# A fused attention and feed-forward kernel: a pair of short blocks handled two pairs later, two squares moved between engines, and another order for the first block

## Chip, cores, metric

One core of a Trainium2 chip. The metric is the device time of one execution in microseconds (us), lower is better. Executions of this kernel scatter by about 1%, so differences of a few tenths of a per cent are read from traces, not from times. A trace's span is about 2 us shorter than the time of the same execution.

## The reference, cut to what matters

```python
# q, k, v: (8 batches, 8 heads, 576 positions, 64); x: 4608 tokens x 512
scores = scale * q @ k.T            # kept where 0 <= row - col < 64, else -1e9
attn = softmax(scores); y = attn @ v
x = y.transpose(0, 2, 1, 3).reshape(B * S, H * D)
h = np.maximum(x @ w_in, 0.0)       # w_in 512 x 2048
out = (h * h) @ w_out               # w_out 2048 x 512
```

A sequence of 576 positions is four blocks of 128 and one last block of 64. The last blocks of all eight sequences are gathered into two *pairs* of 128-token tiles (`TAILS`); a pair is 256 tokens, and there are 18 pairs.

## The kernel before: the parts that matter

Two pairs form a group of 512 tokens. Groups 0 and 1 are handled by a hand-written list of words, `FIRST`: `fk0` fetches the keys of pair 0, `kc1/D` casts keys of tile 1 on VectorE, `Tk0`/`ck0` transpose them and copy them out, `S0` makes the scores of tile 0, `V0` multiplies with the values, `X0`/`x0` make xT (the transposed activations), `w3.0` scales a quarter of w_in, `U0.7` is one projection of pair 0, `O` an output product, `W9` nine warm-up matmuls. The order of the words is the order on each engine and in the DMA queue. Every load, store and DMA transpose is issued by one queue, SyncE's, in that order.

From then on each *stage* g projects group g (`UP`), finishes group g-1 by a product scheme with sums on VectorE (`hsum`), does the attention of group g+1 and loads still later pairs. I number stages by g: stage 2 runs from its first `UP` to that of stage 3, and so on to stage 8.

```python
def UP(g, f):
    hps = ps_up.tile([P, 512], FP32, name="hps", tag="ps_u")      # two banks, used in turn
    for c in range(DMC):
        nc.tensor.matmul(hps[:], w_in_sb[:, c, f * P:(f + 1) * P], xT_of(g)[:, :, c, :], ...)   # L526
    hrelu = hrp.tile([P, 512], FP32, name="hrelu", tag="hrelu")
    nc.scalar.activation(out=hrelu[:], in_=hps[:], func=AF.Relu)                                # L530
    if f in SQ_ACT:         # the square reads hrelu alone: the bank is free after the relu
        later(2 if f == 0 else 0, lambda: nc.scalar.activation(
            out=h2_of(g)[:, f, :], in_=hrelu[:], func=AF.Square))                               # L533
    else:                   # the square reads hps too: the bank is free after the square
        nc.vector.scalar_tensor_tensor(out=h2_of(g)[:, f, :], in0=hps[:], scalar=0.0,
            in1=hrelu[:], op0=ALU.max, op1=ALU.mult)                                            # L536
...
# loads(p): dma_k, dma_q are the DMA transposes of keys and queries; load() fetches and casts
ev.append((t + 0.06, lambda a=a: (dma_k(a), dma_q(a))))
ev.append((t + 0.14, lambda a=a, x=kq: load(a + 1, x)))
ev.append((t + 0.3, lambda a=a, x=kq: load(a + 1, "kqv"[len(x):])))
...
# a pair of TAILS: 4 loads of keys, 4 of queries, 4 of values instead of 2, 2, 2;
# three DMA transposes instead of two; two stores (each the last 64 rows of two sequences) instead of one of 256 rows
```

The softmax here doesn't subtract the row's maximum and nothing guards it: scores larger than these inputs give would overflow.

## Time and profile before

| what | value |
|---|---|
| time | 297.83 us median of three (296.83 to 298.15) |
| profiled execution | 299.22 us, span 297.3 us: a longer one than those |
| TensorE | 96% busy, full clock |
| first projection (L498) | 19.85 us |
| first `UP` of stage 2 | 78.62 us |
| stages 2 to 7 | 32.24, 29.25, 28.88, 28.88, 29.88, 28.87 us |

The page of the kernel before: the engines' busy time, TensorE's busy tenths and granted clock in 40 slices, and the chain of waits by engine.

```profile
PE 284.6 (96%) x3042; PEld 196.5 (66%) x3042; DVE 218.8 (74%) x396; ACT 189.9 (64%) x300; POOL 119.7 (40%) x172
...
PE   4999999999989999999999999999999999999995
...
PEclk9999999999999999999999999999999999999999
...
PE 60%; DVE 16%; ACT 8%; DMA 7%; SPq 6%; issue 2%; POOL 1%; POOLq 0%
```

TensorE is nearly always busy, but only 60% of the chain that sets the time runs over it. The rest is where something else let it go on. The waits view of TensorE, before (what waited, on what: us in total, times, longest):

```profile
PE hps L526 <- DVE h L536: 3.1, 5, 1.0
PE warm L545 <- DVE mask_first L249: 2.7, 1, 2.7
PE kT_ps L373 <- DVE k L269: 1.6, 1, 1.6
...
PE sc L425 <- DMA qT<-q: 0.2, 1, 0.2
```

The largest wait after the start-up is `UP` on a VectorE square. One of the five in the timeline (start, duration, engine, line, operation, and in brackets the idle time before it and who ended it):

```profile
113.70 1.09 DVE L436 TENSOR_TENSOR pm<-pm,mask_inner 128x1024 f16<-128x1024 f16 x1
114.71 1.09 DVE L602 TENSOR_TENSOR hs_all<-h 128x1024 f16<-128x1024 f16 x1
115.84 0.69 DVE L602 TENSOR_TENSOR hs_all<-hs_all,h 128x1024 f16<-128x1024 f16 x1
116.45 0.68 DVE L536 SCALAR_TENSOR_TENSOR h<-hps,hrelu 128x512 f16<-128x512 f32 x1
...
113.86 0.59 ACT L530 ACTIVATE hrelu<-hps 128x512 f32<-128x512 f32 x1
115.43 0.60 ACT L530 ACTIVATE hrelu<-hps 128x512 f32<-128x512 f32 x1 [0.98 <-PE hps L526]
...
117.19 1.89 PE L526 MATMUL hps<-xT,w_in_sb 128*128 128x512 f16 x8 [0.29 <-DVE h L536]
```

The relu of f=1 (113.86) ended at 114.45, but its square stood behind a mask and two sums and ended at 117.13; only then could the next-but-one projection take the bank. ScalarE was idle for 0.98 us in between. (The view prints 0.29 us of idle; from the start of the matmul before, the gap over its own streaming time was 0.45. "By gaps" below means that.)

Last, the issuing queue around the start of stage 6 (197.87 us) in the kernel before, timeline of SyncE:

```profile
190.36 1.23 SPq L477 DMA_TRANSPOSE xT<-x_sb  x1
191.64 3.73 SPq L121 DMA_DIRECT2D kq_st<-in_q_dram  x4
195.41 3.54 SPq L121 DMA_DIRECT2D kq_st<-in_v_dram  x4
199.07 1.72 SPq L645 DMA_DIRECT2D out_dram<-osb_all  x2
200.88 0.73 SPq L651 DMA_DIRECT2D out_dram<-osb_all  x1
201.72 4.85 SPq L397 DMA_TRANSPOSE kT<-k  x2
206.66 2.20 SPq L397 DMA_TRANSPOSE qT<-q  x1
```

These follow one another without a gap. The last landed at 210.84 us, and the scores of that tile waited for it. I call the time from the start of the xT transpose to that landing the *stretch*: here 20.5 us.

One thing more is in the timeline at 113.70 to 116.5, and I overlooked it when I predicted: of operations of one shape (128x1024, fp16), some took 1.09 us and some 0.69.

### The profile page before, as it was taken

How to read it: one execution, taken by the hardware profiler on the slowest of the kernel's cores; microseconds unless marked ns; L12 is line 12 of the kernel's file. 1: busy time of each engine (PE TensorE's matmuls, PEld its weight loads, DVE VectorE, ACT ScalarE, POOL GpSimd, SP SyncE). 2: the span in 40 equal slices, each digit the busy share in tenths (PEclk: the TensorE clock that was granted, in tenths of full speed). 3: DMA queues.
4: the chain of work that ended last, by engine and by line, in shares of the span. 5: the costliest groups of instructions: out<-in, count | busy, mean ns of one | idle time of the engine just before them, and what ended most of it. 6: DMA issues, size and time to landing. Idle time of an engine off the chain costs nothing.

```text
span 297.3 us, 7475 instructions
## 1 busy us (share of the span) xinstructions
PE 284.6 (96%) x3042; PEld 196.5 (66%) x3042; DVE 218.8 (74%) x396; ACT 189.9 (64%) x300; POOL 119.7 (40%) x172
## 2 busy tenths in 40 slices
PE   4999999999989999999999999999999999999995
PEld 3667878855656566666666666665666566666684
DVE  4568799798889569684978597868676966645393
ACT  2669999885574756757675667575757575566500
POOL 2304878758416266555364626233275300000000
PEclk9999999999999999999999999999999999999999
DMA  7998999995789999868996989989999701300133
GB/s 222 279 390 274 276 268 350 317 262 151 193 139 241 197 296 225 184 144 252 208 207 145 235 189 202 164 187 204 232 205 308 131 13 35 143 0 0 73 106 108
DMA packets 151842, 57.64 MB, mean 194 GB/s; under 512 B 128256, under 2 KB 143616, under 8 KB 151808
## 3 DMA queue, kind: packets, MB, share of 16 engines
q1 hardware_dynamic: 151808, 57.16, 79.5%
q8 instruction: 24, 0.39, 0.5%
q14 instruction: 10, 0.08, 0.1%
HBM read 38.80 MB, written 9.44 MB: 162 GB/s over the span
## 4 chain that ended last, share of the span: by engine, by line
PE 60%; DVE 16%; ACT 8%; DMA 7%; SPq 6%; issue 2%; POOL 1%; POOLq 0%
PE hps L526 26%; PE opsC L614 9%; PE opsD L614 8%; PE opsA L614 4%; PE opsB L614 4%; DMA wb_all<-in_moe_w_in_dram 4%; DVE hs_all L602 4%; SPq L121 3%; DVE pm L436 3%; PE hps L498 2%; PE av L448 2%; ACT pm L431 2%; PE sc L425 2%; SPq L130 2%; ACT h L517 1%
## 5 line engine op out<-in xcount | busy, mean ns | idle before, releaser
L526 PE MATMUL hps<-xT,w_in_sb 128*128 128x512 f16 x448 | 112.8, 379 | 3.1 <-DVE h L536 3.1
L530 ACT ACTIVATE hrelu<-hps 128x512 f32<-128x512 f32 x112 | 66.7, 597 | 70.6 <-PE hps L526 70.6
L614 PEld LDWEIGHTS <-h 128*128 128x128 f16 x624 | 60.4, 98 | 20.7 <-issue 0.2
L526 PEld LDWEIGHTS <-w_in_sb 128*128 128x128 f16 x448 | 42.6, 98 | 35.7 <-issue 3.3
L536 DVE SCALAR_TENSOR_TENSOR h<-hps,hrelu 128x512 f16<-128x512 f32 x56 | 38.6, 689 | 29.0 <-ACT hrelu L530 28.6
L269 POOL COPY v_od<-v_ev 64x512 f16<-64x512 f16 x51 | 39.0, 765 | 6.7 <-ACT v_ev L267 3.5
L431 ACT ACTIVATE pm<-sc 128x1024 f16<-128x1024 f32 (+1 forms) x40 | 35.3, 937 | 3.3 <-PE sc L425 3.3
L533 ACT ACTIVATE h<-hrelu 128x512 f16<-128x512 f32 x56 | 35.2, 629 | 1.5
L614 PE MATMUL opsA<-w_out_sb,h 128*128 128x256 f16 x240 | 31.0, 273 | 0.0
L614 PE MATMUL opsD<-wb_all,h 128*128 128x256 f16 x240 | 30.9, 273 | 0.0
L498 PE MATMUL hps<-xT,w_in_sb 128*128 128x256 f16 x256 | 30.6, 273 | 0.3 <-DVE xT L269 0.2
L614 PEld LDWEIGHTS <-hs_all 128*128 128x128 f16 x256 | 25.0, 98 | 8.7
L498 PEld LDWEIGHTS <-w_in_sb 128*128 128x128 f16 x256 | 24.0, 98 | 4.1 <-DVE xT L269 0.5
L457 DVE TENSOR_TENSOR x_sb<-av,rden 128x512 f16<-128x512 f32 x36 | 24.9, 691 | 1.2
L436 DVE TENSOR_TENSOR pm<-pm,mask_inner 128x1024 f16<-128x1024 f16 x25 | 21.1, 847 | 6.0 <-ACT pm L431 5.9
L269 POOL CAST k<-kq_st 128x512 f16<-128x512 f32 x18 | 11.9, 662 | 27.2 <-DMA kq_st<-in_k_dram 26.8
L269 POOL CAST q<-kq_st 128x512 f16<-128x512 f32 x22 | 15.4, 701 | 17.0 <-DMA kq_st<-in_q_dram 16.7
L269 POOL CAST v_ev<-kq_st 128x512 f16<-128x512 f32 x16 | 11.0, 686 | 21.3 <-DMA kq_st<-in_v_dram 14.9
L636 DVE SCALAR_TENSOR_TENSOR osb_all<-opsD,u 128x512 f32<-128x512 f32 x14 | 9.7, 690 | 11.3 <-PE opsD L614 11.3
L614 PE MATMUL opsC<-w_out_sb,h 128*128 128x256 f16 x128 | 16.4, 273 | 0.0
L614 PE MATMUL opsB<-wb_all,hs_all 128*128 128x256 f16 x128 | 16.4, 273 | 0.0
L614 PE MATMUL opsC<-w_out_sb,hs_all 128*128 128x256 f16 x128 | 16.4, 273 | 0.0
(102 smaller groups left out, 378.5 us busy)
## 6 DMA issues: line engine op xcount, KB each, us to landing
kq_st<-in_k_dram SPq DMA_DIRECT2D x26, 256.0 KB, 3.7
kq_st<-in_v_dram SPq DMA_DIRECT2D x24, 256.0 KB, 3.7
out_dram<-osb_all SPq DMA_DIRECT2D x12, 512.0 KB, 4.1
kq_st<-in_q_dram SPq DMA_DIRECT2D x18, 256.0 KB, 4.3
v_st<-in_v_dram SPq DMA_DIRECT2D x16, 256.0 KB, 5.3
k_st<-in_k_dram SPq DMA_DIRECT2D x7, 512.0 KB, 5.5
q_st<-in_q_dram SPq DMA_DIRECT2D x7, 512.0 KB, 6.2
out_dram<-osb_all SPq DMA_DIRECT2D x11, 256.0 KB, 2.5
```

Of the source, the lines that this page charges most:

```text
L269: eng.tensor_copy(out=out, in_=in_)
L431: nc.scalar.activation(out=pms[i][:, part], in_=scs[i][:, part], func=AF.Exp, scale=1.0 / float(D) ** 0.5)
L436: nc.vector.tensor_tensor(out=pms[i][:, part], in0=pms[i][:, part], in1=mask[:].rearrange("p (o a) r -> p o (a r)", o=1) .to_broadcast([P, ...
L457: nc.vector.tensor_tensor(out=xs[i // 2][:, i % 2], in0=avs[i][:, :, :, 0:D], in1=rden[:].to_broadcast([P, 2, 4, D]), op=ALU.mult)
L498: nc.tensor.matmul(hps[:, f, :], w_in_sb[:, c, (2 * j + f) * P:(2 * j + f + 1) * P], xT_of(p // 2)[:, n0:n0 + 2, c, :], start=(c == 0), st ...
L526: nc.tensor.matmul(hps[:], w_in_sb[:, c, f * P:(f + 1) * P], xT_of(g)[:, :, c, :], start=(c == 0), stop=(c == DMC - 1))
L530: nc.scalar.activation(out=hrelu[:], in_=hps[:], func=AF.Relu)
L533: later(2 if f == 0 else 0, lambda: nc.scalar.activation(out=h2_of(g)[:, f, :], in_=hrelu[:], func=AF.Square))
L536: nc.vector.scalar_tensor_tensor(out=h2_of(g)[:, f, :], in0=hps[:], scalar=0.0, in1=hrelu[:], op0=ALU.max, op1=ALU.mult)
L602: nc.vector.tensor_tensor(out=Sh[i][:, ks], in0=x[:, ks], in1=y[:, ks], op=op)
L614: nc.tensor.matmul(rows_of(bank, m), a[:, kk, m * P:(m + 1) * P], w[:, kk], start=(first and kk == 0 and (m == 0 or bank in apart)), stop= ...
L636: nc.vector.scalar_tensor_tensor(out=dst, in0=banks[bank][:, ms], scalar=OUT_SCALE, in1=sums[add][:, ms], op0=ALU.mult, op1=ALU.add)
```

## The change

Three parts: the first pair of last blocks goes from pair 8 to pair 10; in each stage f=1 is squared on ScalarE instead of f=2 (in stage 2, f=2 and f=9 are too); and `FIRST` is reordered.

```diff
-SQ_ACT = (0, 2, 4, 6, 8, 10, 12, 14)
+SQ_ACT = (0, 1, 4, 6, 8, 10, 12, 14)
-        if f in SQ_ACT:
+        if f in SQ_ACT or g == 2 and f in (2, 9):
-    TAILS = (8, 15)
+    TAILS = (10, 15)
 FIRST = '''
-fv3 fk0 fk1 W9 vc3 fq0 kc0/D kc1/A fq1 h0 vd3/D Tk0 W3 kc3/A kc2 fv1 ck0 Tk1 W8 qc0 qc1/D fv0 h2
-ck1 Tq0 W11 fv2 cq0 qc2/A fw3 qc3/D S0 fw2 vc1/D fw1 S1 W5 ea0 fw0 vc0/D eb0 vd0/D ea1 vc2 vd1/D
+fv3 fk0 fq0 W10 fv0 kc1/D kc0 fq1 Tk0 W1 fv1 qc1/A qc0 vc3/A Tq0 W6 vc0/D h0 vd0 cq0 fv2 ck0 fk1
+qc2/A S0 S1 W2 vc1 ea0 fw3 vd3 fw2 eb0 vd1/D ea1 fw1 V0 W5 qc3/D eb1 vc2 fw0 h2 n0 vd2 V1 Tq1 W7
 ... (all further lines of FIRST are reordered as well; the words are the same but for
      the warm-up counts, 39 matmuls for 42, and some engine letters)
```

More of the change, by code (lines that the diff above doesn't have):

```diff
@@ L13 @@
 ALU = mybir.AluOpType
-SQ_ACT = (0, 2, 4, 6, 8, 10, 12, 14)
+SQ_ACT = (0, 1, 4, 6, 8, 10, 12, 14)
 FIRST = '''
-fv3 fk0 fk1 W9 vc3 fq0 kc0/D kc1/A fq1 h0 vd3/D Tk0 W3 kc3/A kc2 fv1 ck0 Tk1 W8 qc0 qc1/D fv0 h2
-ck1 Tq0 W11 fv2 cq0 qc2/A fw3 qc3/D S0 fw2 vc1/D fw1 S1 W5 ea0 fw0 vc0/D eb0 vd0/D ea1 vc2 vd1/D
-V0 eb1 Tq1 vd2 n0 cq1/A V1 W3 n1 X0 W3 x0 X1 S3 x1/A w3.0 w3.3/A fq2 w3.1 S2 w3.2 ea3 eb3 U0.6 ea2
-V3 eb2 U0.7 n3 w2.1/A w2.3/A w2.0 V2 w2.2 r0.6 X3 n2 U0.5 r0.7 s0.6/A s0.7 X2 U0.4 x2/A x3 w1.0/P
@@ L22 @@
-r0.5/D U1.4 r0.4 h4 s0.5 fk2 w1.3/A U1.7 w1.1/P r1.4/D s0.4/A U1.6 w1.2 s1.4/A r1.7/D U1.3 w0.3/A
-w0.2 s1.7/A U1.2 w0.0 fv4 r1.6 w0.1 U1.5 r1.3 s1.6 r1.2 qc4 fv5 U0.2 r1.5 s1.2 qc5 s1.3/A s1.5 fk3
-kc4 kc5/A Tq2 r0.2 Tk2 vc4 fq3 cq2/A U0.1 ck2/D vd4 U1.1 r0.1 fq4 s0.2 vc5 s0.1/A S4 r1.1/D S5 vd5
-e4 U0.0 h6 e5 U0.3 kc7 m4 fv6 r0.0 m5 V4 s1.1/A qc7 fv9 V5 n4 r0.3 U1.0 qc6 s0.0/A n5 fq5 X4 qc8
-qc9/A Tq3 x4 r1.0 kc6 X5 s0.3 Tq4 fv7 x5/A vc6 Tk3 s1.0 cq3/A U2.5 vd6 ck3/D fk4 cq4/A U2.0 r2.5/D
-S7 r2.0/D S6 e7 U2.2 fv8 s2.5 fo0 vc9/A U2.7 s2.0 e6 vc7 m7 fo1 U2.1 vd7 fo2 r2.2 m6 fo3 U2.4 qc10
@@ L28 @@
-s2.2/A h8 r2.1/D qc11/A kc9 V7 V6 r2.7 n7 vc8 U2.3 s2.7/A vd9 n6 s2.1/A U2.6 r2.3 r2.4/D kc8 X7 X6
-x7 Tq5 s2.4/A vd8 x6 Tk4 s2.3/A r2.6/D U3.7 ck4 s2.6 o2 U3.6 o0 cq5 r3.7 fv10 o1 s3.7/A S9 S8 r3.6
-U3.0 s3.6/A U3.2 e9 r3.0/D o4 U3.4 o7 s3.0/A m9 o3 e8 U3.1 r3.2/D U3.3 s3.2/A m8 o10 r3.1 h10
-r3.4/D O0.0 o5 fv15 s3.1 s3.4/A o6 V8 V9 o8/A O2.0 n9 o9/A fk5 O3.0 n8 o15 o12/A o14/A o11 fk6
-O0.1 ws0.0 vc10/A ws0.1 X9 o13/A h12 O3.1 vd10 r3.3/D fv14 ws0.2 X8 O3.2 ws1.1 ws0.3 O0.2 kc10
-kc11/A x9 ws1.0 s3.3/A O2.1 ws1.3 fv12 ws1.2 ws2.3 O3.3 x8 fq6 ws2.2 kc12 kc13/A Tk5 ws2.0 O2.2
@@ L34 @@
-vc15/A ws2.1 fv11 vc14/A ck5/D Tk6 O0.3 vd14 ck6 fv13 O2.3 oe0 st0 vc12 S11 vd15 oe2/D st2 S10 e11
-U3.5 qc13 fkq14 qc12 e10 O1.0 m11 vc11 O1.1 r3.5 m10 vd11 Tq6 vc13 V10 cq6/A V11 vd12 n10 O1.2
-fkq15 n11 O1.3 qc14 s3.5 X10 kc14 oe1 st1 X11 x10 oe3 st3 vd13 x11 kc15 qc15
+fv3 fk0 fq0 W10 fv0 kc1/D kc0 fq1 Tk0 W1 fv1 qc1/A qc0 vc3/A Tq0 W6 vc0/D h0 vd0 cq0 fv2 ck0 fk1
+qc2/A S0 S1 W2 vc1 ea0 fw3 vd3 fw2 eb0 vd1/D ea1 fw1 V0 W5 qc3/D eb1 vc2 fw0 h2 n0 vd2 V1 Tq1 W7
+n1 kc2/A kc3 cq1 Tk1 X0 W8 ck1 x0 X1 S2 x1/A fv4 w3.0 w3.3/A S3 w3.1 ea2 w3.2 eb2 U0.7 ea3 V2 eb3
@@ new lines @@
+w2.2 U0.6 w2.3/A n2 w2.0/A V3 w2.1 r0.7 X2 n3 U0.5 r0.6 s0.7/A x2 X3 h4 U0.4 r0.5 x3 fk2 w1.0
+s0.6/A U1.7 w1.1 w1.3/A s0.5 U1.5 r0.4 r1.7/D s0.4/A fq2 U1.6 w1.2 r1.5 s1.7 w0.0/A U0.2 w0.2 vc4
+fv5 s1.5/A r1.6/D U1.3 r0.2 s1.6 w0.1/A kc5 U1.2 w0.3 fq3 r1.3 kc4 U1.4 s0.2/A r1.2/D qc5 qc4/A
+s1.3 Tk2 s1.2/A fk3 vd4 Tq2 ck2/D r1.4 U1.1 cq2/A vc5 fq4 U0.1 s1.4 vd5 r1.1/D S4 S5 r0.1/D fv6 e4
+U0.0 qc7 s1.1 qc6 e5 U1.0 m4 kc7 fv9 s0.1/A V4 m5 Tq3 r0.0 fv7 n4 qc8 V5 s0.0/A U0.3 qc9 n5 r1.0
+fq5 kc6 s1.0/A X4 X5 vc6 x4 Tq4 x5/A h6 Tk3 cq3 r0.3 U2.0 fk4 ck3 s0.3 U2.5 vc7 cq4/A r2.0/D fv8
@@ new lines @@
+S7 vd6 s2.0 S6 e7 U2.7 h8 r2.5/D fk5 vc9 U2.6 e6 m7 vd7 fv13 r2.7/D U2.1 r2.6 m6 s2.5/A fo0 vc8 V7
+s2.7/A V6 fo1 n7 qc11 U2.4 s2.6/A fo2 qc10 n6 r2.1 fo3 U2.3 kc11 kc9/A s2.1 X6 kc8 r2.3 X7 x6 U2.2
+vd8 s2.3/A x7 r2.4/D U3.1 r2.2/D vd9 s2.4/A Tk4 r3.1/D s2.2/A Tq5 s3.1 U3.7 ck4 U3.0 vc13/A r3.7/D
+cq5/A fv15 U3.2 vd13 r3.0/D o3/A s3.0 S8 S9 o2 r3.2 s3.7 U3.3 o0 e9 o1 U3.6 r3.3/D s3.2/A o5 U3.4
+s3.3/A r3.6/D o4 e8 s3.6 U3.5 m9 o7/A O2.0 o9 m8 o6/A o8 fv10 O0.0 r3.4 h10 r3.5/D o11 s3.4/A V9
+s3.5/A V8 n9 O0.1 o10/A fv12 ws0.0 O2.1 o12/A n8 fk6 vc15 o13/A O1.0 kc10 ws0.2 X8 fv14 o15 X9
@@ L37 @@
+ws1.0 O2.2 x9/A vc10 x8/A vd15 O1.1 fq6 o14/A Tk5 vc12/A O3.0 ck5/D fv11 O2.3 ws0.1 ws1.2 S10 vc14
+ws0.3 S11 e10 O1.2 kc13 h12 ws1.3 vd10 fkq15 kc12/A O0.2 ws2.0 e11 Tk6 O1.3 ws1.1 vc11/A ws2.3 m10
+ck6 O3.1 vd11 m11 O0.3 qc13/A fkq14 ws2.2 oe1 st1 V10 qc12/A V11 qc15 n10 O3.2 oe2 st2 vd14 kc15/A
+n11 O3.3 ws2.1 vd12 Tq6 oe0/D st0 oe3 st3 X10 X11 cq6/A x10 x11 qc14 kc14
 '''
```

## The prediction

> **What bounds the kernel now.** TensorE: 96% busy on the page, at full granted clock. Busy time overstates this (the Trainium skill, "Trainium Kernel Development and Optimization", Performance Expectations: matmuls are pipelined), so I read start-to-start gaps. In the chain of waits four 512-column matmuls of L526 take 0.86 us, 216 ns each; the skill's "TensorE: Matmul & The Clock Gate", Back-to-back issue gap, gives N/2.4+2.5 = 216 ns: the trace agrees. In steady stages TensorE streams at its rate; only its waits can be won. The change removes no matmul but three warm-up ones.
>
> Its waits over 0.15 us (timeline, waits view):
> - Five times L526 waits for a square on VectorE (L536) to free its PSUM bank, 3.1 us in the waits view, 3.9 us by gaps: at 85.7 us (1.18), 100.3 (0.62), 117.2 (0.45), 204.6 (0.86), 234.4 (0.77). Four are the square of f=1 at a stage's start, queued behind four L602 sums and two masks; one is f=9 of the first stage.
> - First block, from its first projection (19.85 us) to 78.6: 2.8 us in seven waits (w_in casts, xT at 25.7, keys at 32.8, masks at 37.5 and 38.5, kT at 71.2).
> - 0.34 us for a qT transpose DMA at 211.0.
>
> **What the change does, costed.**
> 1. f=1 to ScalarE (0.63 us; 0.69 on VectorE), f=2 back. The bank of f=1 is free after its relu; ScalarE idles 1.0 us just there. Square 2 comes on VectorE right behind the sums (done about 117.1; UP4 needs it at about 117.6): no new wait. In the first stage f=2 and 9 go to ScalarE too. Gain: 1.6 us (first stage), 0.45 (117), 0.75 (234). At 204.6 nothing: the DMA queue is busy without a break from the xT transpose at 190.36 over loads, stores and three transposes until qT lands at 210.84. TensorE then waits 1.2 there instead of 0.34 us. Sum 2.8 us.
> 2. Last-block pair from 8 to 10: twelve loads (some 10 us of queue, 85.7 to 95.6) and three transposes move one stage later, where xT goes by DMA. Estimate from those durations: its second xT transpose is issued at 134.3 instead of 132.6, lands by 138; UP needs it at 140. No gain, no loss, little margin.
> 3. First-block order: the same 3 MB precede w_in, so its quarters land as before (18.2, 22.5, 25.2 us); the first projection cannot start much before 19.4. Gain where xT of pair 1 and keys/queries of pair 2 come sooner, and w1 casts leave GpSimd (1.5 us each). I take half of the 2.8 us: 1.4.
>
> Total 4.2 us, less slippage: 3.8, all on TensorE's own chain.
>
> **Predicted: 294.0 us, 292.0 to 296.6 in 8 of 10 cases** (1.3% faster). Faster by over 2% 0.10, within 2% 0.88, slower by over 2% 0.02.
>
> **What would show it.** Waits view: L526 <- L536 falls from 3.1 us to under 0.6; S <- DMA qT rises to about 1.2 near 207; the first L526 stage (78.6 to 110.9) shrinks from 32.2 to about 30.6 us; stages without a wait (28.9 us) stay; the first block ends about 1.4 us earlier (77.2).
>
> **What would make it wrong.** xT landing late through the moved last blocks (new wait near 139); a first-block order starving on pair 1's keys, now loaded eighth (2 us either way); square 2 blocking the bank of UP4; the DMA chain at 190 to 211 following TensorE after all (0.9 us more gain).

## The result, and the profile after

The changed kernel took 294.38 us (median of 4 runs, 293.98 to 295.43), the kernel before 297.53 us in the same comparison (4 runs). The ratio is 0.990, 95% interval 0.9863 to 0.9938. A ratio here is the mean time of one kernel's runs over that of the other's of the same rounds, so it isn't quite the ratio of the medians. Executions over 1.5% slower than the fastest of the same kernel are left out of the means.

The page after, the same lines:

```profile
PE 283.1 (97%) x3039; PEld 195.5 (67%) x3039; DVE 211.6 (73%) x392; ACT 192.3 (66%) x304; POOL 112.7 (39%) x171
...
PE 87%; DVE 4%; DMA 4%; SPq 2%; ACT 1%; issue 1%
```

TensorE's share of the chain rose from 60 to 87%: it is now held up by little else. Its waits view, after, in full:

```profile
PE warm L545 <- DVE mask_first L249: 2.7, 1, 2.7
PE kT_ps L373 <- POOL k L269: 1.6, 1, 1.6
PE kT_ps L373 <- ACT k L267: 0.4, 1, 0.4
PE hps L526 <- DMA xT<-x_sb: 0.4, 1, 0.4
```

The waits of `UP` on squares are gone, and the one on qT too. A new one is there, `UP` on the xT transpose, at 222.9 us. The start of stage 3 in the timeline after:

```profile
109.70 0.59 ACT L530 ACTIVATE hrelu<-hps 128x512 f32<-128x512 f32 x1
110.33 0.63 ACT L533 ACTIVATE h<-hrelu 128x512 f16<-128x512 f32 x1
...
111.92 0.69 DVE L536 SCALAR_TENSOR_TENSOR h<-hps,hrelu 128x512 f16<-128x512 f32 x1 [1.03 <-ACT hrelu L530]
...
112.69 1.90 PE L526 MATMUL hps<-xT,w_in_sb 128*128 128x512 f16 x8
```

ScalarE squares f=1 at 110.33 in time that it had idle. VectorE's first square is now f=2, and the projections at 112.69 follow the attention without a bracket: no wait.

Where the span went, from the timelines of all traces with a full profile (us; the last column is the time from the first `UP` of stage 8 to the end, 40.7 in all of them):

| kernel | first L498 | first `UP` | st. 2 | st. 3 | st. 4 | st. 5 | st. 6 | st. 7 | span |
|---|---|---|---|---|---|---|---|---|---|
| before | 19.85 | 78.62 | 32.24 | 29.25 | 28.88 | 28.88 | 29.88 | 28.87 | 297.33 |
| changed | 19.02 | 76.30 | 30.45 | 28.91 | 28.94 | 28.88 | 29.42 | 28.20 | 291.82 |
| again | 19.48 | 76.38 | 30.46 | 29.19 | 28.93 | 28.88 | 29.14 | 28.20 | 291.90 |
| again2 | 18.93 | 76.42 | 30.45 | 29.24 | 28.93 | 28.94 | 28.88 | 28.20 | 291.78 |
| squares | 19.55 | 77.95 | 30.45 | 28.93 | 28.88 | 28.88 | 30.85 | 28.20 | 294.87 |
| tails | 20.41 | 78.78 | 32.36 | 29.76 | 28.89 | 28.88 | 30.04 | 28.20 | 297.65 |
| first | 18.67 | 75.41 | 31.26 | 28.89 | 28.92 | 28.88 | 30.09 | 28.20 | 292.38 |
| no_tails2 | 19.57 | 76.78 | 30.46 | 28.88 | 28.92 | 28.88 | 28.90 | 28.20 | 291.75 |
| stores_later | 20.05 | 76.88 | 30.46 | 28.88 | 28.92 | 28.88 | 29.16 | 28.28 | 292.20 |
| xt_ahead | 19.46 | 76.92 | 30.46 | 28.88 | 28.92 | 28.93 | 28.88 | 28.28 | 292.00 |
| best | 18.56 | 75.54 | 30.46 | 28.88 | 28.92 | 28.88 | 29.04 | 28.54 | 290.99 |
| q1_last | 20.60 | 78.64 | 31.83 | 28.91 | 28.88 | 28.88 | 29.13 | 28.60 | 295.59 |
| loads_old | 23.18 | 80.53 | 30.46 | 29.54 | 28.93 | 28.93 | 28.93 | 28.25 | 296.30 |

The two traces first compared differ by 5.5 us, the medians by only 3.15: the trace of before is of a 299.2 us execution, the one of after of the fastest of four. So no sum taken from that pair of traces alone is the effect of the change; that is what the repeats in the table are for. (Stage 7 without a wait takes 28.20 us, the stages before it 28.88.)

### The profile page after: what moved, and what is told of

The parts are those of the page before. It is cut to its first block, busy times and chain, and to the rows that moved or that the text cites. A ratio compares the mean times of both kernels' runs of the same rounds, so it can differ in the third digit from the quotient of the medians.

```text
span 291.8 us, 7469 instructions
## 1 busy us (share of the span) xinstructions
PE 283.1 (97%) x3039; PEld 195.5 (67%) x3039; DVE 211.6 (73%) x392; ACT 192.3 (66%) x304; POOL 112.7 (39%) x171
## 4 chain that ended last, share of the span: by engine, by line
PE 87%; DVE 4%; DMA 4%; SPq 2%; ACT 1%; issue 1%
PE hps L526 33%; PE opsC L614 10%; PE opsA L614 9%; PE opsD L614 8%; PE hps L498 7%; PE ops L574 5%; PE opsB L614 5%; PE av L448 4%; PE sc L425 3%; DMA k_st<-in_k_dram 2%; DMA xT<-x_sb 2%; SPq L121 1%; SPq L130 1%; DVE hrelu L508 1%; PE xt_ps L468 1%; DVE pm L436 1%
## 5 line engine op out<-in xcount | busy, mean ns | idle before, releaser
L536 DVE SCALAR_TENSOR_TENSOR h<-hps,hrelu 128x512 f16<-128x512 f32 x54 | 37.2, 689 | 33.8 <-ACT hrelu L530 33.6
L533 ACT ACTIVATE h<-hrelu 128x512 f16<-128x512 f32 x58 | 36.5, 629 | 1.6
L498 PE MATMUL hps<-xT,w_in_sb 128*128 128x256 f16 x256 | 30.3, 273 | 0.1
L498 PEld LDWEIGHTS <-w_in_sb 128*128 128x128 f16 x256 | 24.2, 98 | 3.2 <-issue 0.3
L457 DVE TENSOR_TENSOR x_sb<-av,rden 128x512 f16<-128x512 f32 x36 | 24.9, 691 | 1.2
L269 POOL CAST k<-kq_st 128x512 f16<-128x512 f32 x17 | 10.7, 634 | 32.4 <-DMA kq_st<-in_k_dram 32.3
L436 DVE TENSOR_TENSOR pm<-pm,mask_inner 128x1024 f16<-128x1024 f16 x25 | 19.2, 770 | 5.0 <-ACT pm L431 4.9
L269 POOL CAST q<-kq_st 128x512 f16<-128x512 f32 x22 | 14.7, 670 | 18.1 <-DMA kq_st<-in_q_dram 17.9
```

The source lines that it names most:

```text
L269: eng.tensor_copy(out=out, in_=in_)
L436: nc.vector.tensor_tensor(out=pms[i][:, part], in0=pms[i][:, part], in1=mask[:].rearrange("p (o a) r -> p o (a r)", o=1) .to_broadcast([P, ...
L457: nc.vector.tensor_tensor(out=xs[i // 2][:, i % 2], in0=avs[i][:, :, :, 0:D], in1=rden[:].to_broadcast([P, 2, 4, D]), op=ALU.mult)
L498: nc.tensor.matmul(hps[:, f, :], w_in_sb[:, c, (2 * j + f) * P:(2 * j + f + 1) * P], xT_of(p // 2)[:, n0:n0 + 2, c, :], start=(c == 0), st ...
L533: later(2 if f == 0 else 0, lambda: nc.scalar.activation(out=h2_of(g)[:, f, :], in_=hrelu[:], func=AF.Square))
```

## Experiments

Four kernels of a set ran on one chip beside the kernel before, five rounds each.

### The three parts, one at a time

**squares**: the kernel before with

```diff
-SQ_ACT = (0, 2, 4, 6, 8, 10, 12, 14)
+SQ_ACT = (0, 1, 4, 6, 8, 10, 12, 14)
-        if f in SQ_ACT:
+        if f in SQ_ACT or g == 2 and f in (2, 9):
```

> The kernel before with only the squares moved (f=1 to ScalarE for f=2, and f=2 and 9 of the first stage). If the three parts are independent (theory A): the five waits of L526 on L536 go, stage one shrinks from 32.2 to about 30.6 us, the third-last wait (204.6) turns into a longer wait of S on the qT transpose DMA (0.34 to about 1.2 us), so 2.8 us less: about 0.991 of before. Rival B (the tails and the squares need one another): with the last-block pair still in stage one, the first stage does not reach 30.8 us.

Ratio 0.994 (0.9895 to 0.9985), where about 0.991 was expected. Stage 2 shrank from 32.24 to 30.45 us, the same as in the changed kernel, with the last blocks still at pair 8; rival B falls. But stage 6 grew to 30.85. TensorE's waits in this run:

```profile
PE sc L425 <- DMA qT<-q: 1.1, 1, 1.1
...
PE hps L526 <- DMA xT<-x_sb: 0.7, 1, 0.7
```

By gaps the scores wait 1.24 us for qT at 208.4, as expected, and then `UP` of stage 7 waits 0.83 us for xT at 225.9, which nobody expected. With the waits on squares gone TensorE runs ahead, and the DMA queue, which it had not seen before, becomes what it waits for.

**tails**: the kernel before with `TAILS = (10, 15)`.

> The kernel before with only the last-block pair moved from 8 to 10. Theory A: no gain by itself, ratio 0.998 to 1.002; the waits on L536 stay near 3 us. If the two 64-row stores that left the queue between 190 and 211 us were what shortened that stretch (20.5 us before, 19.1 after, from the xT transpose to the landing of qT), it is about 19.5 us here and the 0.34 us wait on qT is gone. If the shortening was chance, it stays near 20.5.

Ratio 1.0019 (0.9975 to 1.0062): no gain, as expected. The waits on squares fell to 1.8 us although no square moved (below). The stretch took 19.5 us and the wait on qT is gone. In exchange, TensorE's waits show the new one:

```profile
PE hps L526 <- DVE h L536: 1.8, 3, 1.0
PE hps L526 <- DMA xT<-x_sb: 1.4, 2, 0.8
```

The wait at 117 us went with GpSimd's work beside it. Busy time of TensorE, its weight loads, VectorE, ScalarE and GpSimd (us, with the number of instructions) in six microseconds at the start of stage 3, before and in `tails`:

```profile
111.00:117.00 6.00, 5.90 (x69) 4.01 (x67) 5.88 (x7) 4.66 (x9) 4.12 (x6) 1.00 1.11 228
```

```profile
111.30:117.30 6.00, 6.00 (x69) 4.02 (x68) 4.76 (x9) 4.66 (x8) 0.00 (x0) 1.00 0.95 225
```

With the last-block pair at 8, its loads stand before those of the next pair, and GpSimd was still casting and copying that pair's values until 115.3 us; in `tails` it had done so by 106.1. It was busy for 4.12 us of the six before and not at all in `tails`, and the two masks and four sums in front of the square of f=1 took 5.64 us before and 4.13 in `tails`. In the four kernels with the old squares (before, `tails`, `first`, `q1_last`), the start of stages 3 to 7 has a wait on this square in every case where these six operations took 5.5 us or more (5.52 us: 0.36, three times; 5.64: 0.45; 5.67: 0.51; 5.94: 0.78; 6.02: 0.86), and none over 0.13 us where they took 5.3 or less. No run took GpSimd's work away and left all else, so the slowing is read from the traces, not tested by itself.

One of the two waits on xT is at 140.9 us (0.85 by gaps). With twelve loads and three transposes of the moved pair in stage 3, its second xT transpose was issued at 136.60 us. That is the danger which the prediction named, and which it judged to be just avoided.

**first**: the kernel before with the new `FIRST` alone.

> The kernel before with only the new first-block order. Theory A: the DMA queue ran dry just before w_in in the order of before (161 GB/s at 12 to 13 us where the changed kernel moves 347), so w_in quarters land at about 17.2, 19.9, 22.6, 25.2 as in the changed kernel and the first L526 stage starts at 76.3 instead of 78.6: ratio about 0.992. Rival: the later landing in the one trace of before was chance of that execution (it was a slow one, 299.2 us); then the landings here scatter and the gain is about 1.4 us, ratio 0.995.

Ratio 0.9927 (0.9887 to 0.9968). The first `UP` comes at 75.41 us. The w_in quarters landed at 16.5, 19.7, 22.4 and 25.1 us. In the three traces with the old order (before, squares, tails) they landed at 17.6 to 18.2, 20.3 to 22.5, 23.0 to 25.1 and 27.2 to 27.8. So the earlier landing of the last quarter is a property of the order; of the second quarter's 22.45 in the first trace, some was chance. Stage 2 also shrank by 1.0 us and the wait at 117 us vanished, with the old squares (the six masks and sums took 5.28 us): the parts overlap.

**again**: the changed kernel itself.

> The changed kernel itself on the same chip as its three parts. Theory A: ratio 0.99, the sum of the parts within 0.002. Its trace repeats the wait of 0.5 us on the xT transpose near 223 us if that is a property of the order and not of one execution, and w_in lands again at 17.2 to 25.2 us.

Ratio 0.9898 (0.9859 to 0.9938). The wait on xT near 223 was not repeated (0.21 us on something else there), but one of 0.31 us at 136.0 came, on xT. w_in landed at 16.9 to 25.0.

What follows: squares and first-block order make up the gain. The product of their ratios is 0.994 times 0.9927, or 0.987, the changed kernel 0.990: nothing is left for the moved pair to give, as far as ratios known to 0.004 each can tell.

### What the moved last blocks are worth, and by what

**no_tails**: the changed kernel with

```diff
-    TAILS = (10, 15)
+    TAILS = (8, 15)
```

> The changed kernel with the last-block pair put back to 8, so squares and first-block order only. Theory (the pair's own stores are the link): three stores stand in the DMA queue between the xT transpose and the three transposes of pair 15, that stretch takes 20.3 to 20.6 us as in every run with the pair at 8, S waits about 1.1 us on qT, and the stage lasts about 30.8 us instead of 29.2: ratio to before about 0.994 against 0.990 of the changed kernel. Rival (tails do nothing for the time, as I predicted): ratio 0.990, stage near 29.4.

Ratio 0.9881 (0.985 to 0.9913) of its five runs; my expectation of 0.994 was wrong. Its profile fell on a sixth execution of 578.98 us, and can't be compared (see the last section). So I ran it again beside the changed kernel:

> The kernel of no_tails again, because the profile of no_tails fell on an execution at half TensorE speed (577 us) and its five fast runs gave 0.988, not the 0.994 that I expected. If moving the pair is worth nothing in sum (its gain at the qT wait is paid elsewhere, or the qT wait is shorter here than in the squares run), the ratio is again within 0.003 of the changed kernel's beside it, and the trace shows what stage 6 (near 194 to 223 us) waits for: with theory 'queue stretch' 1.1 us on qT; otherwise under 0.5 us.

> The changed kernel on the same chip as no_tails2, for a direct comparison. Ratio 0.990. If the last-block pair is worth 1.4 us, no_tails2 is at 0.994 to 0.995; if nothing, both are equal within 0.002.

no_tails2: 293.45 us, ratio 0.987 (0.9844 to 0.9897). again2: 293.85 us, ratio 0.9887 (0.9869 to 0.9904). Moving the pair is worth nothing that times can show, and the medians lean the other way. The trace of no_tails2 has no wait over 0.2 us after 46 us, and stage 6 takes 28.90 us: here the stretch took 19.2 us.

**stores_later**: no_tails with the two 64-row stores of pair 8 put behind the three transposes.

```diff
-                        nc.sync.dma_start(            # a store of 64 rows, twice
+                        later(10 if g == 4 else 0, lambda n=n, b0=b0: nc.sync.dma_start(
```

> As no_tails, but the two 64-row stores of pair 8 are issued behind the three transposes of pair 15 instead of before them; nothing else moves. If those stores are the link, the stretch from the xT transpose to qT falls below 19.5 us, the wait on qT falls to under 0.2 us, with a ratio near the changed kernel's 0.990. If something else of the moved pair shortened the stretch (loads, buffers), it stays at 20.3 or more and the wait at about 1.1 us.

Ratio 0.9878 (0.9849 to 0.9907). The queue in that stage, timeline of SyncE:

```profile
194.57 0.80 SPq L651 DMA_DIRECT2D out_dram<-osb_all  x1
195.47 3.62 SPq L397 DMA_TRANSPOSE kT<-k  x2
199.19 1.26 SPq L397 DMA_TRANSPOSE qT<-q  x1
200.54 1.94 SPq L645 DMA_DIRECT2D out_dram<-osb_all  x2
```

The stretch fell to 17.0 us (17.2 in `best`, which has the same order), and no wait on qT is left. (A wait of 0.29 us on a square, at 202.86 us, is there instead.) So the stores in front of the transposes do lengthen it by about 2 us or more. But they are not enough to make TensorE wait every time. All stretches measured: with the pair at 8 and the stores in front 20.5, 20.6, 20.3, 19.2 and 19.4; with the pair at 10 19.5, 19.1, 19.2, 18.6, 18.8 and 18.4. TensorE does not wait when it is below about 19.5 us (21.64 us of its own work from the attention before to those scores, less the 2.0 us from that attention to the xT transpose, less some 0.1 us from landing to start). With the pair at 8 the stretch lies on both sides of that line, from execution to execution; at 10 it lies below or on it. What makes it vary by over 1 us with the same program is not settled.

**xt_ahead**: the changed kernel with the loads of keys and queries of pairs 11 and 17 behind the xT transpose of their stage.

```diff
-ev.append((t + 0.14, lambda a=a, x=kq: load(a + 1, x)))
+ev.append((t + (0.28 if a in (10, 16) else 0.14), lambda a=a, x=kq: load(a + 1, x)))
```

> The changed kernel with the loads of keys and queries of pairs 11 and 17 issued behind the second xT transpose of their stage instead of before it. If the waits of 0.2 to 0.5 us that remain at 136 and 223 us come from those four loads standing before that transpose (about 3.9 us of queue), both waits vanish, no new one over 0.3 us comes, and the trace is 0.3 to 0.6 us shorter; ratio about 0.9885. If the transpose is late for its data, nothing changes.

Ratio 0.9883 (0.9858 to 0.9909). No wait on xT is left; stages 3 and 6 take 28.88 us each. That alone would prove little, since without this edit the first trace after has no wait at 136 us and again2 none at 223. But the queue shows it: in the changed kernel it issued those four loads without a break up to the transpose at 131.57 us; here it had nothing to issue from 127.55 to 128.76 us, when the data came and the transpose was issued. The mechanism holds: these four loads held up the transpose, not its data. The span, 292.0 us, is not shorter than the changed kernel's 291.8, because this execution lost 0.5 us more in the first block. So the gain is seen in the stages alone.

### The first block: loads or order of work

**q1_last**: the kernel before with the queries of pair 1 loaded just before w_in.

```diff
-fv3 fk0 fk1 W9 vc3 fq0 kc0/D kc1/A fq1 h0 ...
+fv3 fk0 fk1 W9 vc3 fq0 kc0/D kc1/A h0 ...
-ck1 Tq0 W11 fv2 cq0 qc2/A fw3 qc3/D S0 ...
+ck1 Tq0 W11 fv2 fq1 cq0 fw3 S0 ...
-V0 eb1 Tq1 ...
+V0 eb1 qc2/A qc3/D Tq1 ...
```

> The kernel before with the 512 KB load of queries of pair 1 moved behind three 256 KB value loads, so that it is the last before w_in; its two casts move behind the first exponentials. If the DMA queue ran dry before w_in because three loads of 256-byte rows stood there, the throughput at 12 to 14 us stays over 280 GB/s, the first w_in quarter lands near 17.2 instead of 18 and the last near 25.2 instead of 27.4. If the earlier landing in the changed kernel needs the keys and queries of pair 0 first, w_in lands as before.

Busy time by stretches; the two last columns are the DMA engines' mean busy share and GB/s. (The share adds up the times of all packets that start in the stretch, so it can exceed 1.) Before:

```profile
12.00:13.00 1.00, 1.00 (x9) 0.55 (x6) 1.00 (x2) 0.00 (x0) 0.00 (x0) 1.00 0.85 161
13.00:14.00 1.00, 1.00 (x25) 0.50 (x26) 0.97 (x4) 0.52 (x2) 0.64 (x1) 1.00 0.79 240
```

The changed kernel:

```profile
12.00:13.00 1.00, 1.00 (x22) 0.74 (x21) 0.97 (x3) 0.96 (x2) 0.87 (x3) 1.00 1.20 347
13.00:14.00 1.00, 1.00 (x27) 0.89 (x26) 0.97 (x3) 0.00 (x0) 0.96 (x2) 1.00 0.96 352
```

q1_last:

```profile
11.00:12.00 1.00, 1.00 (x10) 0.88 (x8) 0.30 (x1) 0.00 (x0) 0.36 (x1) 1.00 0.79 194
12.00:13.00 1.00, 1.00 (x11) 0.90 (x10) 1.00 (x2) 0.00 (x0) 0.89 (x3) 1.00 1.01 280
13.00:14.00 1.00, 1.00 (x21) 0.40 (x18) 1.00 (x3) 0.13 (x1) 0.79 (x1) 1.00 1.01 351
```

From 12 to 14 us the rate is up, as the dry-queue theory has it, but part of the dip has only moved forward: 194 GB/s at 11 to 12 us, against 233 before and 264 in the changed kernel. From 11 to 14 us the DMA engines moved 0.63 MB before, 0.83 here and 0.96 in the changed kernel. w_in landed at 17.5, 20.3, 23.0 and 25.7 us, the last quarter some 2 us earlier. How much of those 2 us is the dip's doing is not clear (see loads_old). And the time did not fall: ratio 1.0026 (0.9996 to 1.0057), first projection at 20.60, first `UP` at 78.64 us. This is no clean test of an earlier w_in, for the moved queries came late themselves: TensorE waited 0.77 us for their cast at 16.50. It shows that an earlier w_in did not make the first projection earlier.

**loads_old**: the changed kernel with its first eight loads in the order of before, all else as changed.

```diff
-fv3 fk0 fq0 W10 fv0 kc1/D kc0 fq1 Tk0 W1 fv1 qc1/A ... cq0 fv2 ck0 fk1 ...
+fv3 fk0 fk1 fq0 W10 fq1 kc1/D kc0 fv1 Tk0 W1 fv0 qc1/A ... cq0 fv2 ck0 ...
```

> The changed kernel with the first eight loads in the order of before (keys of pair 1 third, three value loads last), all else as changed. If the load order is what won 2.4 us in the first block, the first projection starts at about 19.9 instead of 19.1 us, the last w_in quarter lands at about 27.4 instead of 25.2, and the first L526 stage starts near 78 (ratio 0.995). If the order of the work on the engines won it, the stage starts at about 76.5 as changed although w_in lands late (ratio 0.991).

Neither came: 298.45 us, ratio 1.004 (1.0015 to 1.0065). TensorE's timeline there: the queries of pair 0, the first scores, and the first projection.

```profile
9.37 1.03 PE L373 MATMUL qT_ps<-ident,q 128*128 128x128 f16 x8 [1.65 <-POOL q L269]
13.78 0.61 PE L425 MATMUL sc<-qT,kT 64*128 64x64 f16 x16 [1.24 <-DVE qT L269]
...
23.18 1.05 PE L498 MATMUL hps<-xT,w_in_sb 128*128 128x256 f16 x8
```

The first two of these in the changed kernel's timeline:

```profile
10.45 0.41 PE L425 MATMUL sc<-qT,kT 64*128 64x64 f16 x16
...
19.02 1.05 PE L498 MATMUL hps<-xT,w_in_sb 128*128 128x256 f16 x8
```

A dip is back (206 GB/s at 12 to 13 us), but a smaller one: 0.81 MB from 11 to 14 us, where the three traces before, squares and tails moved 0.63 to 0.67. So the order of the loads is only part of it. w_in landed at 17.8, 20.5, 23.2 and 25.8 us. In the eight traces with the new `FIRST` the last quarter landed at 24.9 to 26.1 us, so no cost of the dip can be read from 25.8; why the last quarter came at 27.2 to 27.8 us in those three traces stays open.

The first quarter was there at 17.8 us, yet the first projection came only at 23.18. What sets it is the attention of the first tiles, and two loads that it needs came late. The queries of pair 0 were put back by one load of 512 KB: TensorE transposed them at 9.37 us, 1.5 later than in the changed kernel (7.86). The values of tile 0 were put back from fourth to seventh place, and on VectorE their cast stands in front of the copy of the transposed queries:

```profile
12.01 0.43 DVE L269 CAST v_ev<-v_st 128x512 f16<-128x512 f32 x1 [6.07 <-DMA v_st<-in_v_dram]
...
12.49 1.23 DVE L269 COPY qT<-qT_ps 128x1024 f16<-128x1024 f16 x1
```

That copy began at 8.93 us in the changed kernel. Both together put the first scores off by 3.3 us and the first projection by 4.2. From the first projection on, loads_old needs 57.35 us to the first `UP` (80.53 less 23.18), the changed kernel 57.28, the kernel before 58.77. Over all traces in the table it is 56.7 to 57.5 us with the new order of work and 58.0 to 58.8 with the old. So the order of the work on the engines wins about 1.3 us there, with either order of loads. The first projection itself comes 0.7 us earlier on average (18.6 to 20.1 us in the eight traces with the new `FIRST`, 19.6 to 20.4 in before, squares and tails); the three warm-up matmuls fewer, all of them before it, may be up to 0.6 us of that (an estimate: three times the 213 ns from one early warm-up to the next), which no run tests. The old loads under the new work lose; the new loads under the old work were not run.

### A version of both

**best**: squares and new first block, the pair at 8, its stores behind the transposes, and the loads for pair 17 behind the xT transpose.

```diff
-    TAILS = (10, 15)
+    TAILS = (8, 15)
-                        nc.sync.dma_start(            # a store of 64 rows, twice
+                        later(10 if g == 4 else 0, lambda n=n, b0=b0: nc.sync.dma_start(
-ev.append((t + 0.14, lambda a=a, x=kq: load(a + 1, x)))
+ev.append((t + (0.28 if a == 16 else 0.14), lambda a=a, x=kq: load(a + 1, x)))
```

> Squares and first-block order with the pair at 8, its two stores issued behind the three transposes, and the last keys and queries loaded behind the second xT transpose. If queue order alone is what the move of the pair helped, no stage after the first has a wait over 0.3 us, all inner stages last 28.9 us, and the time is at or below the changed kernel: ratio 0.987 to 0.990.

292.83 us, ratio 0.9856 (0.9833 to 0.9878), against 0.9887 (0.9869 to 0.9904) of the changed kernel beside it. It is the fastest kernel, clearly faster than the kernel before. That it beats the changed kernel by 0.3% is likely but not established: the intervals overlap, and in its trace the inner stages are not shorter (stage 7 has a new wait of 0.34 us on a square, more than the 0.3 that I had allowed); the lead there comes from the first block, which is the same program in both.

## Why the prediction was right, and where it wasn't

The time was predicted at 294.0 us and measured at 294.38. Point by point:

- *TensorE bounds the kernel, only its waits can be won.* Right. Stages without a wait take 28.9 us in nearly every trace, and TensorE's share of the chain rose from 60 to 87%.
- *Stage 2 from 32.2 to about 30.6 us by the squares.* Right: 30.45, with the squares alone too.
- *0.45 us at 117 and 0.75 at 234 by the squares.* The waits went, but they are not the squares' to win alone. The wait at 117 is absent in `first` and in `tails`, and that at 234 too, with the old squares. What I had not seen is that the masks and sums in front of the square have no fixed length: they took 5.64 and 5.94 us at 117 and 234 before, but 4.13 in `tails` and 5.28 and 5.24 in `first`, according to what GpSimd did meanwhile, and below about 5.3 us the old square is in time. In the first trace after, those of stage 3 took 4.1 us, so there the old squares would probably not have waited either; in `squares` they took 5.6 and the new squares did not wait. The new squares have a limit too: in stores_later and `best`, where the six took 5.9 us, `UP` of f=5 waited 0.29 and 0.34 us for the square of f=3. That is close to what the prediction named as a danger; none of the three traces of the changed kernel shows it.
- *At 204.6 nothing, for the queue then makes S wait 1.2 us.* For the squares alone this was right to the number (1.24 us). In the changed kernel it was wrong: no wait on qT, stage 6 shorter by 0.5 to 1.0 us over three traces. The step that failed is "Last-block pair from 8 to 10 ... No gain, no loss": I followed the pair's loads and transposes and overlooked its two stores, which had stood in that very stretch. Putting them elsewhere cut the stretch from 19 to 20.5 us to 17. In part it is scatter: no_tails2 had the stores in place and no wait.
- *xT lands by 138, UP needs it at 140; little margin.* Here the margin was gone more often than not: waits of 0.85, 0.31 and 0.36 us in `tails`, `again` and `again2`, none in the first trace after. This eats what the pair's move gives in stage 6. The sum, no gain and no loss, stands by no_tails2 and again2, though by two effects that cancel rather than by none.
- *First block 1.4 us.* Too small: 2.3 us (78.62 to 76.30), over all pairs of a trace with the old `FIRST` and one with the new (loads_old and q1_last aside) 1.0 to 3.4. What the 1.4 counted, waits removed after the first projection, came about: that part is 1.3 us shorter on average. The step that failed is "the same 3 MB precede w_in, so its quarters land as before ... the first projection cannot start much before 19.4". The first projection started 0.7 us earlier on average, in four of eight traces before 19.1. The quarters landed 1.0 to 2.6 us earlier in the first pair of traces; the cause is open, and the dip is at most a part of it. And w_in was not what the first projection waited for: q1_last and loads_old had it early, and started at 20.60 and 23.18 us.
- *The total.* 3.8 us expected, 3.15 by the medians. That the terms missed in both directions helped: that the total came so close is in part luck.

## What to carry to other kernels

When you remove waits from the busiest engine, list what else has slack in the same stretch, the issuing queue above all: count every instruction in it, stores included, and see how many microseconds it has left before the engine will wait for it. Read the durations of the operations in front of a late one, not only their order: here the same sum on VectorE took 0.69 or 1.1 us with GpSimd idle or at work. Reordering loads and reordering the work that uses them are one change; half of it can be slower than neither. Compare several traces of each version before explaining a difference of a microsecond, since waits at the edge come and go from one execution to the next.

## What the Trainium skill lacked or had wrong

- "TensorE: Matmul & The Clock Gate", Part 1: The HAM clock gate, has the array at half rate when cold and at full rate after one busy window of about 3.4 us. The page warns that its clock events can be unreliable and that the gate has been seen stuck at a quarter for over 50 us; a whole execution at half rate is not in it. One execution of no_tails ran at half rate from start to end under dense matmuls, 578.98 us long: 443 ns from one 512-column matmul to the next (median) against 216 in other runs; the page's cold figure, 512/1.2, is 427 ns. ScalarE's relu had its usual duration (597 ns). The profile's granted clock (mean 0.973) does not show it; the spacing does. Why this one execution ran so is not known. First line: a projection in no_tails, second fence: one in the changed kernel.

```profile
201.42 2.05 PE L526 MATMUL hps<-xT,w_in_sb 128*128 128x512 f16 x4
```

```profile
106.75 1.03 PE L526 MATMUL hps<-xT,w_in_sb 128*128 128x512 f16 x4
```

- "DMA: Bandwidth & Descriptors", Issuing engines are not separate DMA queues, calls the time to initiate a DMA "usually small relative to the DMA itself". Here it added up: of the 20.5 us of the stretch, 16.3 us (190.36 to 206.66) passed in issuing fourteen DMAs one after another. There a DMA transpose held the queue for 1.2 to 3.2 us and took 4.2 to 7.5 from issue to landing, a load of 128 or 256 KB held it for 0.6 to 1.7 us and took 3.1 to 4.2. Whether that is issuing proper or back-pressure from the DMA engines no run tells apart.
- "DMA: Bandwidth & Descriptors", Specifications, gives 512 B as the smallest transfer at line rate. In the first block the value loads have runs of 256 B, keys and queries of 512 B; the trace of before agrees as far as it goes: 287 GB/s at a share of 1.27 while value loads ran (10 to 11 us), 347 at 1.15 for keys and queries (6 to 7 us). What no page that I used has is the dip between these loads and w_in: 161 to 207 GB/s from 12 to 13 us in four traces with three value loads last, at shares of 0.85 to 1.01. Three value loads in a row are not its condition, for in xt_ahead, with a 512 KB load of keys last, the rate fell to 135 GB/s at 11 to 12 us, at a share of 0.61. Its cause is open.
